# Decode attention over 65,536 keys on one core: from a tile framework with 2 MB tiles to hand-written engine programs with 8 MB tiles

## The chip, the core and the metric

The kernel runs on one core of a Trainium2 chip. The core has a matrix engine (TensorE, PE), a vector engine (VectorE, DVE), an activation engine (ScalarE, ACT), a general engine (GpSimd, POOL) and an engine that mostly issues transfers (SyncE, SP). Data comes from device memory (DRAM) into the on-chip buffer (SBUF, 128 partitions) through 16 DMA engines; matmul results land in PSUM, also on the chip. The metric is the device time of one execution in microseconds (us), the median of several runs.

## The reference

32 query heads in 8 groups of 4 share 8 key/value heads. Each head has one query of 128 numbers and looks at 65,536 keys.

```python
B, Hq, Hkv, Sq, Sk, D = 1, 32, 8, 1, 65536, 128      # all bfloat16
k = jnp.repeat(k, 4, axis=1)
v = jnp.repeat(v, 4, axis=1)
scores = jnp.einsum("bhqd,bhkd->bhqk", q, k) * D ** -0.5
p = _softmax(scores, axis=-1)
return jnp.einsum("bhqk,bhkd->bhqd", p, v)
```

Keys and values are 8 x 65536 x 128 x 2 bytes each, together 268.4 MB, and each byte is used once. The output is 8 KB.

## The kernel before

A tile framework orders the work: the program is written in sequence, and the framework puts in the waits between engines and recycles buffers out of pools.

**Tiles and loads.** The 65,536 rows of one group are 512 rows for each of 128 partitions. A tile is 64 rows for each partition, 16 KB a partition and 2 MB in all, so a group has KT = 8 key tiles and 8 value tiles. `k_load` (L117) and `v_load` (L209) issue them from SP into one pool of 8 buffers (`iopool`), keys and values in turn. In the key tensor a partition's rows lie 128 KB after those of the partition before; in the value tensor, which is cut in four parts first, 32 KB. The very last value tile is loaded in 4 pieces of 512 KB (`pieces=4`, L259).

**The order.** The outer loop runs over g = 0..8 (L251). In turn g it does, for s = 0..7, the key tile s of group g (`k_step`) and the value tile s of group g-1 (`v_step`), and then `softmax(g)`. So values run one group behind keys.

**k_step.** For each 16 rows of a key tile DVE transposes 32x32 blocks of 4-byte pairs into a new tile T (L128), and PE does four matmuls of 128x512 with a sparse query matrix `wq` as weights (L140), which add up in PSUM. After 32 matmuls ACT copies 128x512 scores from PSUM to `S_g` in SBUF (L148).

**softmax.** DVE takes the maximum (L153), PE and DVE bring it together and spread it (L157 to L171), ACT does exp with the sum (L175), PE transposes the weights in 16 pieces (L194) and ACT copies them into `ET` (L197).

**v_step.** PE multiplies 4 value rows at a time, 128x512, with 32 columns of `ET` as weights, in four column strips of PSUM in turn (L226). After the last tile of a group ACT copies the sums (L235), 4 matmuls, each run as two passes, pick the wanted parts (L238), DVE divides (L246), and ACT issues the store (L249).

`queries` fills `wq` for a group (L107), on POOL from group 1 on.

Of the kernel before, what the change touches and what calls it, by code (L numbers as in the profile page):

```python
# [8 lines left out]
ALU = mybir.AluOpType  # L9
# [3 lines left out]

NT = 64
NW = 16
# [3 lines left out]
def kernel(  # L19
# [11 lines left out]

    nc = tc.nc
    P = nc.NUM_PARTITIONS
    B, Hq, Sq, D = q.shape
    _, Hkv, Sk, _ = k.shape
    assert B == 1 and Sq == 1 and D == P  # L40
    HPG = Hq // Hkv
    assert HPG == 4 and HPG * Hkv == Hq
    R = Sk // P
    C = R // 4
    assert C == 8 * NW and R % NT == 0 and C % NT == 0
    NU = 4
    KT = R // NT
    WT = NT // NW
    SCALE = float(D) ** -0.5

    fp32 = mybir.dt.float32
    bf16 = mybir.dt.bfloat16

    const = ctx.enter_context(tc.tile_pool(name="const", bufs=1))
    iopool = ctx.enter_context(tc.tile_pool(name="iopool", bufs=8))
    tpool = ctx.enter_context(tc.tile_pool(name="tpool", bufs=4))
    spool = ctx.enter_context(tc.tile_pool(name="spool", bufs=2))
    epool = ctx.enter_context(tc.tile_pool(name="epool", bufs=2))
    opool = ctx.enter_context(tc.tile_pool(name="opool", bufs=2))
    stats = ctx.enter_context(tc.tile_pool(name="stats", bufs=2))  # L60
    psc = ctx.enter_context(tc.tile_pool(name="psc", bufs=3, space=bass.MemoryType.PSUM))
    pse = ctx.enter_context(tc.tile_pool(name="pse", bufs=2, space=bass.MemoryType.PSUM))
    psm = ctx.enter_context(tc.tile_pool(name="psm", bufs=1, space=bass.MemoryType.PSUM))
    pso = ctx.enter_context(tc.tile_pool(name="pso", bufs=2, space=bass.MemoryType.PSUM))


    qn = const.tile([P, D], bf16)
    for a in range(4):
        nc.scalar.dma_start(out=qn[32 * a:32 * a + 32, :], in_=q[0, :, 0, :])  # L69
    qx = const.tile([P, D], bf16)  # L70
    nc.vector.transpose(out=qx[:, :].bitcast(fp32), in_=qn[:, :].bitcast(fp32))

    qv = qx[:, :].rearrange("p (b h r) -> p b h r", b=2, r=2)

    ident = const.tile([P, P], fp32)
    make_identity(nc, ident[:, :])
    ident_bf = const.tile([P, P], bf16)
    nc.vector.tensor_copy(out=ident_bf[:, :], in_=ident[:, :])

    selx = const.tile([P, 32], fp32)  # L80
    nc.vector.tensor_reduce(
        out=selx[:, :], in_=ident[:, :].rearrange("p (j x) -> p x j", x=32), axis=AX.X, op=ALU.max
    )
    sel = const.tile([P, HPG], fp32)
    nc.vector.tensor_reduce(
        out=sel[:, :], in_=ident[:, :].rearrange("p (x h) -> p h x", h=HPG), axis=AX.X, op=ALU.max
    )
    one = const.tile([1, 1], fp32)
    nc.vector.memset(one[:, :], 1.0)

    Wq = []
    for x in range(2):
        wq = const.tile([P, 8 * 516], bf16, name=f"wq{x}")
        (nc.vector if x == 0 else nc.gpsimd).memset(wq[:, :], 0.0)
        Wq.append(wq)

    def queries(g):
        eng = nc.vector if g == 0 else nc.gpsimd  # L100
        wv = Wq[g % 2][:, :].rearrange("p (w x) -> p w x", x=516)
        for a in range(4):
            qd = slice(32 * a, 32 * a + 32)
            for b in range(2):
                for r in range(2):
                    at = 128 * (2 * b + r) + 32 * a
                    eng.tensor_copy(  # L107
                        out=wv[qd, :, at:at + HPG],
                        in_=qv[qd, b, g * HPG:(g + 1) * HPG, r].unsqueeze(1).broadcast_to([32, 8, HPG]),
                    )  # L110

    S_tiles, sc_tiles, ET_tiles, rl_tiles, o_tiles = {}, {}, {}, {}, {}

    def k_load(g, s):
        kn = iopool.tile([P, NT, D], bf16, name="kn", tag="io")
        src = k[0, g].rearrange("(p n) d -> p n d", p=P)
        nc.sync.dma_start(out=kn[:, :, :], in_=src[:, s * NT:(s + 1) * NT, :])  # L117
        return kn

    def k_step(g, s, kn):  # L120
        if s == 0:
            S_tiles[g] = spool.tile([P, NU, 4 * P], fp32, name="S_g")
        wq = Wq[g % 2]
        for x in range(WT):
            wg = s * WT + x
            nu, w = divmod(wg, 8)
            T = tpool.tile([P, NW * D], bf16, name="T")
            nc.vector.transpose(  # L128
                out=T[:, :].bitcast(fp32),
                in_=kn[:, x * NW:(x + 1) * NW, :].rearrange("p n d -> p (n d)").bitcast(fp32),  # L130
            )
            Tv = T[:, :].rearrange("p (n b i r) -> p n b i r", n=NW, b=2, r=2)
            if w == 0:
                sc_tiles[g] = psc.tile([P, 4 * P], fp32, name="sc")
            sc = sc_tiles[g]
            for b in range(2):
                for r in range(2):
                    bp = 2 * b + r
                    at = w * 512 + bp * 128
                    nc.tensor.matmul(  # L140
                        out=sc[:, :],
                        lhsT=wq[:, at:at + 128],
                        rhs=Tv[:, :, b, :, r],
                        start=(w == 0 and bp == 0),
                        stop=(w == 7 and bp == 3),
                    )
            if w == 7:
                nc.scalar.copy(out=S_tiles[g][:, nu, :], in_=sc[:, :])  # L148

    def softmax(g):  # L150
        S_g = S_tiles[g]
        mx = stats.tile([P, 1], fp32, name="mx")
        nc.vector.tensor_reduce(  # L153
            out=mx[:, :], in_=S_g[:, :, :].rearrange("p n c -> p (n c)"), axis=AX.X, op=ALU.max
        )
        psum_t = psm.tile([1, P], fp32, name="psum_t", tag="misc")
        nc.tensor.transpose(out=psum_t[:, :], in_=mx[:, :], identity=ident[:, :])  # L157
        m4 = stats.tile([1, HPG], fp32, name="m4")
        nc.vector.tensor_reduce(
            out=m4[:, :], in_=psum_t[:, :].rearrange("o (x h) -> o h x", h=HPG), axis=AX.X, op=ALU.max  # L160
        )
        mrow = stats.tile([1, P], fp32, name="mrow")
        nc.vector.tensor_scalar_mul(  # L163
            out=mrow[:, :].rearrange("o (x h) -> o x h", h=HPG),
            in0=m4[:, :].unsqueeze(1).broadcast_to([1, 32, HPG]),
            scalar1=-SCALE,
        )
        psum_b = psm.tile([P, 1], fp32, name="psum_b", tag="misc")
        nc.tensor.matmul(out=psum_b[:, :], lhsT=mrow[:, :], rhs=one[:, :], start=True, stop=True)  # L169
        nmb = stats.tile([P, 1], fp32, name="nmb")  # L170
        nc.vector.tensor_copy(out=nmb[:, :], in_=psum_b[:, :])  # L171

        E_g = epool.tile([P, NW, P], bf16, name="E_g")
        lsum = stats.tile([P, 1], fp32, name="lsum")
        nc.scalar.activation(  # L175
            out=E_g[:, :, :].rearrange("p c (i u) -> p u c i", u=NU),
            in_=S_g[:, :, :].rearrange("p u (c i) -> p u c i", c=NW),
            func=ACT.Exp,
            bias=nmb[:, 0:1],
            scale=SCALE,  # L180
            accum_out=lsum[:, 0:1],
        )
        psum_l = psm.tile([HPG, 1], fp32, name="psum_l", tag="misc")
        nc.tensor.matmul(out=psum_l[:, :], lhsT=sel[:, :], rhs=lsum[:, :], start=True, stop=True)  # L184
        rl = stats.tile([HPG, 1], fp32, name="rl")
        nc.vector.reciprocal(out=rl[:, :], in_=psum_l[:, :])  # L186
        rl_tiles[g] = rl

        ET = epool.tile([P, NW * P + 16], bf16, name="ET")
        nc.gpsimd.memset(ET[:, NW * P:], 0.0)  # L190
        for c4 in range(NW // 4):
            pe = pse.tile([P, 4, P], bf16, name="pe")
            for c in range(4):
                nc.tensor.transpose(  # L194
                    out=pe[:, c, :], in_=E_g[:, 4 * c4 + c, :], identity=ident_bf[:, :]
                )
            nc.scalar.copy(  # L197
                out=ET[:, :NW * P].rearrange("p (x c h) -> p c x h", c=NW, h=HPG)[:, 4 * c4:4 * c4 + 4],
                in_=pe[:, :, :].rearrange("p c (x h) -> p c x h", h=HPG),
            )  # L200
        ET_tiles[g] = ET

# [11 lines left out]
    def v_step(g, s, vb):  # L214
        if s == 0:
            o_tiles[g] = pso.tile([P, 4, D], fp32, name="psum_o")
# [34 lines left out]
    for g in range(Hkv + 1):  # L251
        if g < Hkv:
            queries(g)
# [38 lines left out]
```

## Time and profile before

| what | us |
|---|---|
| median of 3 runs (641.66 to 641.91) | 641.76 |
| span of the profiled execution, first to last instruction | 639.9 |
| PE busy / DVE busy / ACT busy in it | 409.9 / 326.1 / 81.2 |

The profile is one execution of its own; its span leaves out what lies before the first and after the last instruction. An engine's busy time is not by itself a reason for the time: what counts is what the last instruction waited for. The page cuts the span in 40 slices of 16 us; a digit is a share in tenths. The row PEclk gives the clock that was granted to PE, and GB/s what the 16 DMA engines moved. The chain of waits goes back from the last instruction to what released it, and so on to the start.

### The profile page before, as it was taken

How to read it: one execution, taken by the hardware profiler on the slowest of the kernel's cores; microseconds unless marked ns; L12 is line 12 of the kernel's file. 1: busy time of each engine (PE TensorE's matmuls, PEld its weight loads, DVE VectorE, ACT ScalarE, POOL GpSimd, SP SyncE). 2: the span in 40 equal slices, each digit the busy share in tenths (PEclk: the TensorE clock that was granted, in tenths of full speed). 3: DMA queues.
4: the chain of work that ended last, by engine and by line, in shares of the span. 5: the costliest groups of instructions: out<-in, count | busy, mean ns of one | idle time of the engine just before them, and what ended most of it. 6: DMA issues, size and time to landing. Idle time of an engine off the chain costs nothing.

```text
span 639.9 us, 5675 instructions
## 1 busy us (share of the span) xinstructions
PE 409.9 (64%) x2280; PEld 157.7 (25%) x2280; DVE 326.1 (51%) x326; ACT 81.2 (13%) x89; POOL 27.4 (4%) x127
## 2 busy tenths in 40 slices
PE   1996875666675765758657487564875558665554
PEld 0332321232222322223222132221322123221221
DVE  4996645455355553555534555435645356354300
ACT  0003100040000400013000220003100032000310
POOL 4002000200002000020000200002000000000000
PEclk9997878868878689887787877878878978879775
DMA  9999999999999999999999999999999999999994
GB/s 369 432 427 427 425 428 429 428 429 426 427 425 428 429 428 425 428 428 429 428 425 429 426 429 427 428 425 429 427 429 429 427 426 425 429 428 430 429 426 186
DMA packets 19146, 268.85 MB, mean 420 GB/s; under 512 B 2352, under 2 KB 2352, under 8 KB 2864
## 3 DMA queue, kind: packets, MB, share of 16 engines
q1 hardware_dynamic: 18864, 268.44, 98.8%
q8 instruction: 18, 0.29, 0.2%
q10 hardware_dynamic: 256, 0.04, 0.0%
q14 instruction: 8, 0.07, 0.0%
HBM read 268.47 MB, written 0.01 MB: 420 GB/s over the span
## 4 chain that ended last, share of the span: by engine, by line
DMA 82%; PE 9%; DVE 4%; issue 3%; ACT 1%; ACTq 0%; DVEq 0%; SPq 0%
DMA vb<-in_v_dram 43%; DMA kn<-in_k_dram 37%; PE sc L140 7%; DVE T L128 3%; DMA qn<-in_q_dram 1%; PE psum_o L226 1%; ACT E_g L175 1%; DVE mx L153 0%; PE psum_f L238 0%; DVE wq L107 0%; PE pe L194 0%; ACTq L69 0%; DVE o_out L246 0%; ACT o_sb L235 0%; ACT S_g L148 0%
## 5 line engine op out<-in xcount | busy, mean ns | idle before, releaser
L140 PE MATMUL sc<-T,wq 128*128 128x512 bf16 x1024 | 314.5, 457 | 159.9 <-DVE T L128 152.8
L128 DVE STREAM_TRANSPOSE T<-kn 128x1024 f32<-128x1024 f32 x256 | 296.3, 1211 | 211.8 <-DMA kn<-in_k_dram 209.3
L140 PEld LDWEIGHTS <-wq 128*128 128x128 bf16 x1024 | 112.5, 112 | 349.9 <-issue 244.7
L226 PE MATMUL psum_o<-vb,ET 128*32 128x512 bf16 x1024 | 73.3, 405 | 12.0 <-DMA vb<-in_v_dram 12.0
L148 ACT COPY S_g<-sc 128x512 f32<-128x512 f32 x32 | 18.7, 585 | 482.3 <-PE sc L140 482.3
L175 ACT ACTIVATE E_g<-S_g,nmb 128x2048 bf16<-128x2048 f32 x8 | 38.7, 4838 | 29.5 <-DVE nmb L171 29.5
L107 POOL COPY wq<-qx 32x32 bf16<-32x32 bf16 x112 | 22.4, 205 | 413.2 <-PE sc L140 402.7
L226 PEld LDWEIGHTS <-ET 128*32 128x32 bf16 x1024 | 23.7, 99 | 57.0 <-issue 43.2
L153 DVE TENSOR_REDUCE mx<-S_g 128x1 f32<-128x2048 f32 x8 | 18.3, 2286 | 20.5 <-ACT S_g L148 20.5
L184 PE MATMUL psum_l<-lsum,sel 128*4 128x1 f32 x16 | 1.5, 165 | 37.5 <-ACT E_g L175 37.5
L197 ACT COPY ET<-pe 128x512 bf16<-128x512 bf16 x32 | 17.8, 587 | 12.2 <-PE pe L194 12.2
L186 DVE RECIPROCAL rl<-psum_l 4x1 f32<-4x1 f32 x8 | 1.2, 155 | 33.7 <-PE psum_l L184 33.7
L194 PE MATMUL pe<-ident_bf,E_g 128*128 128x128 bf16 x128 | 17.5, 304 | 0.8 <-ACT ET L197 0.8
L246 DVE TENSOR_SCALAR o_out<-psum_f,rl 4x128 bf16<-4x128 f32 x8 | 2.6, 330 | 29.9 <-PE psum_f L238 29.9
L194 PEld LDWEIGHTS <-E_g 128*128 128x128 bf16 x128 | 13.6, 140 | 6.5 <-issue 6.1
L238 PE MATMUL psum_f<-o_sb,selx 128*4 128x128 f32 x64 | 9.1, 290 | 5.5 <-ACT o_sb L235 5.5
L184 PEld LDWEIGHTS psum_l<-lsum,sel 128*4 128x4 f32 x16 | 0.7, 84 | 38.6 <-ACT E_g L175 38.6
L235 ACT COPY o_sb<-psum_o 128x512 f32<-128x512 f32 x8 | 4.7, 585 | 27.4 <-PE psum_o L226 27.4
L238 PEld LDWEIGHTS psum_f<-o_sb,selx 128*4 128x4 f32 x64 | 5.1, 90 | 10.9 <-ACT o_sb L235 9.5
L157 PE MATMUL psum_t<-ident,mx 128*1 128x128 f32 x8 | 2.2, 270 | 6.8 <-DVE o_out L246 3.8
L169 PE MATMUL psum_b<-one,mrow 1*128 1x1 f32 x16 | 3.0, 256 | 5.0 <-DVE mrow L163 5.0
L190 POOL MEMSET ET<- 128x16 bf16 x8 | 0.9, 110 | 79.2 <-PE psum_o L226 78.8
(21 smaller groups left out, 20.9 us busy)
## 6 DMA issues: line engine op xcount, KB each, us to landing
kn<-in_k_dram SPq DMA_DIRECT2D x64, 2048.0 KB, 34.2
vb<-in_v_dram SPq DMA_DIRECT2D x63, 2048.0 KB, 34.2
vb<-in_v_dram SPq DMA_DIRECT2D x4, 512.0 KB, 27.0
out_dram<-o_out ACTq DMA_DIRECT2D x8, 1.0 KB
qn<-in_q_dram ACTq DMA_DIRECT2D x4, 8.0 KB, 8.4
```

What stands on the lines that cost most here:

```text
L107: eng.tensor_copy(out=wv[qd, :, at:at + HPG], in_=qv[qd, b, g * HPG:(g + 1) * HPG, r].unsqueeze(1).broadcast_to([32, 8, HPG]),)
L128: nc.vector.transpose(out=T[:, :].bitcast(fp32), in_=kn[:, x * NW:(x + 1) * NW, :].rearrange("p n d -> p (n d)").bitcast(fp32),)
L140: nc.tensor.matmul(out=sc[:, :], lhsT=wq[:, at:at + 128], rhs=Tv[:, :, b, :, r], start=(w == 0 and bp == 0), stop=(w == 7 and bp == 3),)
L148: nc.scalar.copy(out=S_tiles[g][:, nu, :], in_=sc[:, :])
L153: nc.vector.tensor_reduce(out=mx[:, :], in_=S_g[:, :, :].rearrange("p n c -> p (n c)"), axis=AX.X, op=ALU.max)
L169: nc.tensor.matmul(out=psum_b[:, :], lhsT=mrow[:, :], rhs=one[:, :], start=True, stop=True)
L175: nc.scalar.activation(out=E_g[:, :, :].rearrange("p c (i u) -> p u c i", u=NU), in_=S_g[:, :, :].rearrange("p u (c i) -> p u c i", c=NW), ...
L194: nc.tensor.transpose(out=pe[:, c, :], in_=E_g[:, 4 * c4 + c, :], identity=ident_bf[:, :])
L197: nc.scalar.copy(out=ET[:, :NW * P].rearrange("p (x c h) -> p c x h", c=NW, h=HPG)[:, 4 * c4:4 * c4 + 4], in_=pe[:, :, :].rearrange("p c ( ...
L226: nc.tensor.matmul(out=psum_o[qd, :, :], lhsT=ET[:, col:col + 32], rhs=vb[:, x:x + 4, :], start=(j < 4), stop=(j >= R // 4 - 4),)
L235: nc.scalar.copy(out=o_sb[:, :, :], in_=psum_o[:, :, :])
L238: nc.tensor.matmul(out=psum_f[:, :], lhsT=selx[:, HPG * c:HPG * c + HPG], rhs=o_sb[:, c, :], start=(c == 0), stop=(c == 3),)
```

## The change

The framework's order is replaced by five programs, one for each engine, written out with semaphores inside one critical section.

- Loads are 8 MB: NT = 256 rows, 64 KB a partition, two tiles of keys and two of values a group. There are three buffers. `bufA` takes the first half of a group's keys, `bufB` the second, `bufC` both halves of the values of the group before; at the end A and B take the last group's values. SP issues each load behind a wait for the work that frees its buffer (`kdone`, `vdone`). Keys and values both have partitions 128 KB apart.
- The last value tile comes in 7 pieces of 128, 64, 32, 16, 8, 4 and 4 rows, each with a semaphore. The first two are used as before, four rows at a time; the next three one row at a time in four column strips (`quads`); the last two one row at a time straight into the result (`singles`).
- Keys are transposed in place, half a tile (128x8192 pairs) in one instruction (`turn`).
- The four blocks of 128x512 scores stay in four PSUM banks; one exp reads them all. The weights are turned by one DVE transpose in place of 16 PE transposes and 4 ACT copies.
- `wq` is one copy of shifted windows in place of two large ones, filled by 4 POOL copies a group.
- PE's instructions for groups 1 to 7 stand in a loop of 7 turns that counts semaphores down (`take`).

```diff
-NT = 64
-NW = 16
+G = 8
+H = 4
+P = 128
+D = 128
+NT = 256
+W = 8
+C = 16
+SLIDE = P + 4 * (W - 1)
+PIECES = (128, 64, 32, 16, 8, 4, 4)
...
+    bufA, bufB, bufC = (sbuf(n, (P, NT * D), bf16) for n in ("bufA", "bufB", "bufC"))
+    wq = sbuf("wq", (P, 4 * SLIDE), bf16)
+    E = sbuf("E", (P, 4 * 512 + 32), bf16)
...
+    sc = psum("sc", (P, 4 * 512))
+    psum_o = psum("psum_o", (P, 512))
+    psum_s = psum("psum_s", (P, 512))
+    psum_f = psum("psum_f", (P, 512))
+    misc = psum("misc", (P, 512))
...
+        def load(buf, src, s, semaphore, lo=0, n=NT):
+            sp.dma_start(
+                out=buf[:, lo * D:(lo + n) * D],
+                in_=src[:, s * half + lo * D:s * half + (lo + n) * D],
+            ).then_inc(semaphore, 16)
+        load(bufA, kr[0], 0, sA)
+        load(bufB, kr[0], 1, sB)
+        load(bufC, vr[0], 0, sC)
+        for g in range(1, G):
+            sp.wait_ge(kdone, 2 * g - 1)
+            load(bufA, kr[g], 0, sA)
+            if g == 1:
+                sp.wait_ge(kdone, 2)
+                load(bufB, kr[1], 1, sB)
+                sp.wait_ge(vdone, 1)
+                load(bufC, vr[0], 1, sC)
+                continue
+            sp.wait_ge(vdone, 2 * (g - 1))
+            load(bufC, vr[g - 1], 0, sC)
+            sp.wait_ge(kdone, 2 * g)
+            load(bufB, kr[g], 1, sB)
+            sp.wait_ge(vdone, 2 * (g - 1) + 1)
+            load(bufC, vr[g - 1], 1, sC)
+        sp.wait_ge(kdone, 2 * G - 1)
+        load(bufA, vr[G - 1], 0, sA)
+        sp.wait_ge(kdone, 2 * G)
+        at = 0
+        for x, n in enumerate(PIECES):
+            load(bufB, vr[G - 1], 1, sP[x], at, n)
+            at += n
...
+        def turn(buf, x):
+            kv = buf[:, x * half // 2:(x + 1) * half // 2].bitcast(fp32)
+            dve.transpose(out=kv, in_=kv).then_inc(kt, 1)
...
+        n_pes = 0
+        for g in range(G):
+            dve.wait_ge(sA, 16 * (g + 1))
+            turn(bufA, 0)
+            turn(bufA, 1)
+            dve.wait_ge(sB, 16 * (g + 1))
+            turn(bufB, 0)
+            turn(bufB, 1)
+            dve.wait_ge(kdone, 2 * (g + 1))
+            dve.tensor_reduce(out=mx[:, :], in_=sc[:, :], axis=AX.X, op=ALU.max).then_inc(mxs, 1)
+            if g > 0:
+                n_pes += 1
+                dve.wait_ge(pes, n_pes)
+                dve.tensor_scalar_mul(
+                    out=o_out[:, (g - 1) * D:g * D], in0=psum_f[0:H, 0:D], scalar1=rl[:, 0:1]
+                ).then_inc(outs, 1)
+            n_pes += 1
+            dve.wait_ge(pes, n_pes)
+            after(dve.tensor_reduce(
+                out=m4[:, :], in_=misc[0:1, 0:P].rearrange("o (x h) -> o h x", h=H), axis=AX.X, op=ALU.max
+            ))
+            dve.tensor_scalar_mul(
+                out=mrow[:, :].rearrange("o (x h) -> o x h", h=H),
+                in0=m4[:, :].unsqueeze(1).broadcast_to([1, 32, H]),
+                scalar1=-SCALE,
+            ).then_inc(mxs, 1)
+            n_pes += 1
+            dve.wait_ge(pes, n_pes)
+            dve.tensor_copy(out=nmb[:, :], in_=misc[:, P:P + 1]).then_inc(nms, 1)
+            dve.wait_ge(exd, g + 2)
+            dve.transpose(out=E[:, 0:2048], in_=E[:, 0:2048]).then_inc(ets, 1)
+            n_pes += 1
+            dve.wait_ge(pes, n_pes)
+            dve.reciprocal(out=rl[:, :], in_=misc[0:H, P + 4:P + 5]).then_inc(dl, 1)
...
+        for g in range(G):
+            if g > 0:
+                act.wait_ge(vdone, 2 * g)
+                act.copy(out=o_sb[:, :], in_=psum_o[:, :]).then_inc(ocp, 1)
+            act.wait_ge(nms, g + 1)
+            act.activation(
+                out=E[:, 0:2048], in_=sc[:, :], func=ACT.Exp, bias=nmb[:, 0:1], scale=SCALE,
+                accum_out=lsum[:, 0:1],
+            ).then_inc(exd, 1)
+            if g > 0:
+                store(g - 1)
...
+        def take(semaphore, n=1):
+            pe.wait_ge(semaphore, n).then_inc(semaphore, -n)
+        def scores(buf, x, s):
+            take(kt)
+            bank = sc[:, (2 * s + x) * 512:(2 * s + x + 1) * 512]
+            T = buf[:, x * half // 2:(x + 1) * half // 2].rearrange(
+                "p (c w b i r) -> p w b r c i", c=C, w=W, b=2, r=2
             )
...
+            for w in range(W):
+                for b in range(2):
+                    for r in range(2):
+                        at = (2 * b + r) * SLIDE + 4 * (W - 1 - w)
+                        last = pe.matmul(
+                            out=bank, lhsT=wq[:, at:at + P], rhs=T[:, w, b, r],
+                            start=(w + b + r == 0), stop=(w == W - 1 and b + r == 2),
+                        )
+            return last
...
+        def stream(buf, s, lo, n, end):
+            for row in range(lo, lo + n, 4):
+                j = row // 4
+                qd = slice(32 * (j % 4), 32 * (j % 4) + 32)
+                at = column(s, row) // 32 * 32
+                last = pe.matmul(
+                    out=psum_o[qd, :], lhsT=E[:, at:at + 32], rhs=buf[:, row * D:(row + 4) * D],
+                    start=(s == 0 and j < 4), stop=(s == 1 and row >= end - 16),
                 )
...
+            return last
...
+        def pick(start, stop):
+            for x in range(4):
+                last = pe.matmul(
+                    out=psum_f[0:H, 0:D], lhsT=selx[:, H * x:H * x + H], rhs=o_sb[:, x * D:(x + 1) * D],
+                    start=(start and x == 0), stop=(stop and x == 3),
                 )
...
+            return last
+        def maxima():
+            take(mxs)
+            pe.transpose(out=misc[0:1, 0:P], in_=mx[:, :], identity=ident[:, :]).then_inc(pes, 1)
+            take(mxs)
+            pe.matmul(
+                out=misc[:, P:P + 1], lhsT=mrow[:, :], rhs=one[:, :], start=True, stop=True
+            ).then_inc(pes, 1)
+        def sums():
+            take(ets)
+            pe.matmul(
+                out=misc[0:H, P + 4:P + 5], lhsT=sel[:, :], rhs=lsum[:, :], start=True, stop=True
+            ).then_inc(pes, 1)
...
+        take(wqs, 4)
+        scores(bufA, 0, 0)
+        scores(bufA, 1, 0).then_inc(kdone, 1)
+        scores(bufB, 0, 1)
+        scores(bufB, 1, 1).then_inc(kdone, 1)
+        maxima()
+        with pe.Fori(1, G):
+            sums()
+            take(sC, 16)
+            stream(bufC, 0, 0, NT, NT).then_inc(vdone, 1)
+            take(wqs, 4)
+            scores(bufA, 0, 0)
+            scores(bufA, 1, 0).then_inc(kdone, 1)
+            scores(bufB, 0, 1)
+            take(sC, 16)
+            stream(bufC, 1, 0, NT, NT).then_inc(vdone, 1)
+            scores(bufB, 1, 1).then_inc(kdone, 1)
+            take(ocp)
+            pick(True, True).then_inc(pes, 1)
+            maxima()
+        sums()
+        pe.wait_ge(sA, 16 * (G + 1))
+        stream(bufA, 0, 0, NT, NT).then_inc(vdone, 1)
+        at = 0
+        for x in range(2):
+            pe.wait_ge(sP[x], 16)
+            last = stream(bufB, 1, at, PIECES[x], PIECES[0] + PIECES[1])
+            at += PIECES[x]
+        last.then_inc(vdone, 1)
+        def quads(lo, n, start, stop):
+            for row in range(lo, lo + n):
+                qd = slice(32 * (row % 4), 32 * (row % 4) + 32)
+                col = column(1, row)
+                last = pe.matmul(
+                    out=psum_s[qd, 0:D], lhsT=E[:, col:col + 32], rhs=bufB[:, row * D:(row + 1) * D],
+                    start=(start and row < lo + 4), stop=(stop and row >= lo + n - 4),
+                )
+            return last
+        def singles(lo, n, stop):
+            for row in range(lo, lo + n):
+                col = column(1, row)
+                last = pe.matmul(
+                    out=psum_f[0:H, 0:D], lhsT=E[:, col:col + H], rhs=bufB[:, row * D:(row + 1) * D],
+                    start=False, stop=(stop and row == lo + n - 1),
+                )
+            return last
+        pe.wait_ge(sP[2], 16)
+        quads(at, PIECES[2], True, False)
+        at += PIECES[2]
+        pe.wait_ge(ocp, 1)
+        pick(True, False)
+        pe.wait_ge(sP[3], 16)
+        quads(at, PIECES[3], False, False)
+        at += PIECES[3]
+        pe.wait_ge(sP[4], 16)
+        quads(at, PIECES[4], False, True).then_inc(vdone, 1)
+        at += PIECES[4]
+        pe.wait_ge(sP[5], 16)
+        singles(at, PIECES[5], False)
+        at += PIECES[5]
+        pe.wait_ge(ocp, 2)
+        pe.matmul(out=psum_f[0:H, 0:D], lhsT=selq[:, 0:H], rhs=s_sb[:, :], start=False, stop=False)
+        pe.wait_ge(sP[6], 16)
+        singles(at, PIECES[6], True).then_inc(pes, 1)
```

More of the change, by code (lines that the diff above doesn't have):

```diff
@@ L5 @@
 from concourse import mybir
-from concourse.masks import make_identity
 from concourse._compat import with_exitstack
@@ L52 @@
     bf16 = mybir.dt.bfloat16
[L54 to L130, printed above, removed]
-            )
[L132 to L195, printed above, removed]
-                )
[L197 to L201, printed above, removed]
@@ L251, with sbuf @@
-    for g in range(Hkv + 1):
-        if g < Hkv:
-            queries(g)
-        for s in range(KT):
-            if g < Hkv:
-                k_step(g, s, k_load(g, s))
-            if g > 0:
-                last = g == Hkv and s == KT - 1
-                v_step(g - 1, s, v_load(g - 1, s, pieces=4 if last else 1))
-        if g < Hkv:
-            softmax(g)
+    pe, dve, act, pool, sp = nc.tensor, nc.vector, nc.scalar, nc.gpsimd, nc.sync
+    def sbuf(name, shape, dtype=fp32):
+        return nc.alloc_sbuf_tensor(name, list(shape), dtype)
@@ new lines @@
+    ident = sbuf("ident", (P, P))
+    s64 = sbuf("s64", (P, 64))
+    selx = sbuf("selx", (P, 4 * H))
+    selq = sbuf("selq", (P, 32))
+    sel = sbuf("sel", (P, H))
+    one = sbuf("one", (1, 1))
+    mx = sbuf("mx", (P, 1))
+    m4 = sbuf("m4", (1, H))
+    mrow = sbuf("mrow", (1, P))
+    nmb = sbuf("nmb", (P, 1))
+    lsum = sbuf("lsum", (P, 1))
+    rl = sbuf("rl", (H, 1))
+    sc = psum("sc", (P, 4 * 512))
+    psum_o = psum("psum_o", (P, 512))
+    psum_s = psum("psum_s", (P, 512))
+    psum_f = psum("psum_f", (P, 512))
@@ new lines, with sem @@
+    misc = psum("misc", (P, 512))
+    def sem(name):
+        return tc.alloc_semaphore(name)
+    sA, sB, sC = sem("sA"), sem("sB"), sem("sC")
+    sP = [sem(f"sP{x}") for x in range(len(PIECES))]
+    sQ = sem("sQ")
+    sS = sem("sS")
+    kt = sem("kt")
+    kdone = sem("kdone")
+    vdone = sem("vdone")
+    wqs = sem("wqs")
+    cst = sem("cst")
+    mxs = sem("mxs")
+    pes = sem("pes")
+    nms = sem("nms")
+    qps = sem("qps")
+    exd = sem("exd")
+    ets = sem("ets")
+    ocp = sem("ocp")
```

151 lines of the change are left out of this document (96 added, 55 removed).

## The prediction

> **What bounds the kernel now.** I read the page's slices first, then its chain of waits, then windows over chosen stretches.
>
> ```profile
> span 639.9 us, 5675 instructions
> PEclk9997878868878689887787877878878978879775
> GB/s 369 432 427 427 425 428 429 428 429 426 427 425 428 429 428 425 428 428 429 428 425 429 426 429 427 428 425 429 427 429 429 427 426 425 429 428 430 429 426 186
> q1 hardware_dynamic: 18864, 268.44, 98.8%
> q8 instruction: 18, 0.29, 0.2%
> DMA 82%; PE 9%; DVE 4%; issue 3%; ACT 1%; ACTq 0%; DVEq 0%; SPq 0%
> ```
>
> From the second slice to the last but one, transfers never let up. 268.44 MB at 427 GB/s are 628.7 us of the 639.9. The chain agrees: 82% of it is DMA. No compute engine matters until the last slice, so an edit to PE, DVE or ACT alone is worth nothing; only four things can move the time: the start, the rate, a gap between loads, and the tail. The rate in windows (columns: us of the window, busy us of each engine with its number of instructions, clock, DMA share, GB/s):
>
> ```profile
> core 0: us, PE busy (x) PEld busy (x) DVE busy (x) ACT busy (x) POOL busy (x), PEclk, DMA share, GB/s
> 20.00:40.00 20.00, 18.77 (x77) 7.25 (x76) 20.00 (x19) 1.17 (x2) 0.00 (x0) 1.00 1.01 431
> 300.00:500.00 200.00, 131.71 (x727) 49.70 (x725) 99.23 (x92) 21.77 (x25) 6.71 (x34) 0.83 1.01 428
> 624.00:630.00 6.00, 2.64 (x24) 0.96 (x27) 0.00 (x0) 0.00 (x0) 0.00 (x0) 0.50 0.96 391
> 630.00:634.30 4.30, 2.86 (x28) 0.78 (x20) 0.00 (x0) 0.00 (x0) 0.00 (x0) 0.50 0.37 148
> ```
>
> At the end the 16 DMA engines do not finish together. At 428 GB/s the last two windows would carry 4408 KB; they carry 391 x 6 + 148 x 4.3 = 2982 KB. The missing 1426 KB are 3.3 us of full rate. The tail, from the timeline (start, duration, engine, line):
>
> ```profile
> 624.32 1.90 PE L226 MATMUL psum_o<-vb,ET 128*32 128x512 bf16 x16 [3.85 <-DMA vb<-in_v_dram]
> ...
> 631.74 0.62 PE L226 MATMUL psum_o<-vb,ET 128*32 128x512 bf16 x4 [0.15 <-DMA vb<-in_v_dram]
> ...
> 633.00 0.62 PE L226 MATMUL psum_o<-vb,ET 128*32 128x512 bf16 x4 [0.65 <-DMA vb<-in_v_dram]
> ...
> 634.25 0.62 PE L226 MATMUL psum_o<-vb,ET 128*32 128x512 bf16 x4 [0.64 <-DMA vb<-in_v_dram]
> ...
> 634.91 0.59 ACT L235 COPY o_sb<-psum_o 128x512 f32<-128x512 f32 x1 [24.54 <-PE psum_o L226]
> ...
> 635.55 1.87 PE L238 MATMUL psum_f<-o_sb,selx 128*4 128x128 f32 x8 [0.69 <-ACT o_sb L235]
> 637.46 0.34 DVE L246 TENSOR_SCALAR o_out<-psum_f,rl 4x128 bf16<-4x128 f32 x1 [29.86 <-PE psum_f L238]
> 637.83 0.26 ACTq L249 DMA_DIRECT2D out_dram<-o_out  x1
> ```
>
> The last quarter tile releases PE at 634.25. From there to the end of the span are 5.65 us: matmuls, copy, pick, divide, and 2.07 from the store's issue to the end. So the profiled time is 634.25 + 5.65, and the median of the runs, 641.76, is 1.86 above this span; I carry that 1.86 over.
>
> **Part 1: fewer, larger loads.** Before, 64 + 63 whole tiles and 4 quarters are 131 loads; after, 31 whole tiles and 7 pieces are 38. What does one load cost beyond its bytes? Two sizes are in the trace. A 2.097 MB tile at 431 GB/s takes 4.866 us. The 0.524 MB quarters released PE at 631.74, 633.00 and 634.25, so 1.255 us each. The 1.573 MB between the two sizes take 3.611 us, which is 435.6 GB/s; 0.524 MB at that rate are 1.204 us; 0.051 us are left for the load itself, its 128 rows and its completion. With 428 GB/s for the tile the same steps give 0.040. I take 0.051, since in 20 to 40 us the DMA engines still ran evenly, as the quarters' spacing does. 93 loads fewer: -4.7 us. This supposes that a 64 KB row costs no more beside its bytes than a 16 KB row. If the row is cut into 16 KB pieces on its way, most of it is gone and the term is 0; as the other end I take -6, for a price that is a quarter above the row's.
>
> The page "SBUF — State Buffer" of the Trainium skill (section "The DMA setup-cost knee") gives every transfer a fixed cost of about 2 us, which is mostly completion. By that rule 93 fewer loads would save some 186 us as an estimate. The trace disagrees for a full queue: the rows above leave 0.05 us, because the next load's data move while one completes.
>
> **Part 2: three buffers in place of eight.** The queue holds fewer loads; a gap opens if a buffer is not free when the load before it ends. What the waits in the new SP program depend on:
>
> ```profile
> L128 DVE STREAM_TRANSPOSE T<-kn 128x1024 f32<-128x1024 f32 x256 | 296.3, 1211 | 211.8 <-DMA kn<-in_k_dram 209.3
> L71 DVE STREAM_TRANSPOSE qx<-qn 128x64 f32<-128x64 f32 x1 | 0.2, 245 | 7.6 <-DMA qn<-in_q_dram 7.6
> L153 DVE TENSOR_REDUCE mx<-S_g 128x1 f32<-128x2048 f32 x8 | 18.3, 2286 | 20.5 <-ACT S_g L148 20.5
> L175 ACT ACTIVATE E_g<-S_g,nmb 128x2048 bf16<-128x2048 f32 x8 | 38.7, 4838 | 29.5 <-DVE nmb L171 29.5
> L107 POOL COPY wq<-qx 32x32 bf16<-32x32 bf16 x112 | 22.4, 205 | 413.2 <-PE sc L140 402.7
> ```
>
> ```profile
> 15.39 0.14 PEld L140 LDWEIGHTS <-wq 128*128 128x128 bf16 x1 [0.28 <-issue]
> 15.82 0.14 PEld L140 LDWEIGHTS <-wq 128*128 128x128 bf16 x1 [0.28 <-issue]
> ...
> 519.70 2.29 DVE L153 TENSOR_REDUCE mx<-S_g 128x1 f32<-128x2048 f32 x1 [3.67 <-ACT S_g L148]
> ...
> 529.04 0.15 DVE L186 RECIPROCAL rl<-psum_l 4x1 f32<-4x1 f32 x1 [4.07 <-PE psum_l L184]
> ...
> 535.79 3.64 PE L140 MATMUL sc<-T,wq 128*128 128x512 bf16 x16
> 539.36 1.05 PE L226 MATMUL psum_o<-vb,ET 128*32 128x512 bf16 x16
> ```
>
> A transpose of 8192 pairs: from 64 pairs in 0.245 us to 1024 in 1.211 a pair adds 1.006 ns, so 0.245 + 8128 x 1.006 ns = 8.4 us; the other end is eight short ones, 9.7. I take 9. A score matmul takes 3.64 / 16 = 0.23 us at the better clock, 0.43 at the spacing of the early weight loads; half a tile (32) is 7.3 or 13.8. A value tile (64) is 4.2 (from 1.05 / 16), or 7.6 (from 1.90 / 16). From the maximum to the reciprocal, softmax took 529.19 - 519.70 = 9.5 us; its DVE transpose of the weights has no row, and I bound it by 1.2 (as many bytes as a 1024-pair one) and 2.3 (as many elements as the maximum): 12 in all.
>
> An 8.389 MB load takes 19.4. Count from the landing of A(g), and let each engine work in program order. DVE turns A by 9 and 18. The first value half lands at 19.4 and PE has it by 23.6; scores of A end at 38.2, and A is needed again at 58.2. B lands at 38.8, is turned by 48 and 57; its first half is scored by 55. The second value half lands at 58.2 and is used by 62.4; C is needed again at 77.6. B's second half is scored by 70; B is needed at 97. Softmax ends by 82, the next value half lands at 97. So each buffer is free 15 to 27 us early, and the queue does not run dry: 0. DVE's wait for the scores (`kdone`) holds back the next group's transposes, which wait for data until 77.6 anyway; SP's waits hold only loads that no one needs sooner; POOL's `wq` copies (4 x 0.2) lie under the value half. One place is tighter: the last pieces wait for B, free at 70 or, at half clock, at 66 + 13.8 = 80; they should start at 77.6. That is 0, at most +2.4.
>
> At the start A needs 19.4 us to land before any work, and B and C are already queued; A must be free at 58.2 after its start and, by the same durations at half clock, is so at 19.4 + 18 + 13.8 = 51. The longer wait of the first work is covered by the queue; if it were not, each us late would be a us lost. POOL's constants and the query load lie under it as well.
>
> **Part 3: the work that leaves.** The 32 score copies, the 16 weight transposes and 4 copies a group, `S_g` and the pool bookkeeping go: 0, since DMA covers them all. The loop adds branches and may load PE's instructions anew at each turn. The q8 row has 18 such transfers of 0.29 MB in all, and they share the DMA engines with the data. Bounds: the unevenness of 3.3 us vanishes or doubles. I take 0.
>
> **Part 4: the tail.** PE's program after the 64-row piece is short matmuls. The clock is 0.50 in the last windows. For a `quads` matmul (32 weight columns, 128 columns moved) the nearest row is 1.90 / 16 = 0.119 us for four times the columns; a quarter of that is 0.03. I take 0.06, as the weight load doesn't shrink with the columns. After the 32-row piece 1.05 MB are still to come, 2.4 us and four loads, so it lands 2.6 before the last one. Then 32 x 0.06 end at -0.7; `pick` (1.87) at +1.2; 24 more quads at +2.6; the copy of 128 columns, between nothing and the 0.59 for 512, 0.3, at +2.9; the `selq` matmul, two passes of 1.87 / 8, at +3.4; four `singles` at 0.06 at +3.6; divide 0.34 and store 2.07, with hops: +6.2. Against 5.65 that is +0.5. Ends: 2.9 if only the last four matmuls, the divide and the store remain; with 0.119 for 64 matmuls, 10: -2.8 to +4.3.
>
> **Sum.** 639.9 - 4.7 + 0 + 0 + 0.5 = 635.7 us of span, and 637.6 us of time. The start is taken as unchanged: SP issues its first load first, as before.
>
> **The rivals.**
>
> (a) *The row is cut on its way, or the rate doesn't rise.* The 16 KB rows of before say nothing of 64 KB ones. Then 641.8 + 0.5 = 642.3 us, no measurable difference.
>
> (b) *PE becomes the bound, at half clock.* In the new loop PE's work is a chain: values, A, B, values, B, softmax. For it speaks that the PEclk row hardly reaches 9 after the start and that in the new order PE idles for 10 us at a time. At 0.43 us a period is 128 x 0.43 + 128 x 0.119 + 12 for softmax + 1.9 for `pick` + 0.8 = 85 us, against 77.6 for its four loads: 7 turns x 7.4 = 52, so 690 us. It decides from about 0.39 us a matmul on. Against it: bursts of 32 to 64 matmuls, and 0.23 in the burst at 535.79; then the period is 53 us. The Trainium skill's "TensorE: Matmul & The Clock Gate" (Part 1) says that the clock halves after about 3.4 us of idling and comes back after 3.4 us of work. The 0.83 in the window 300 to 500 agrees with clocks in between; by that rule only the start of each burst is slow.
>
> (c) *The queue runs dry at each hand-over*, if the wait before a load passes only after the load ahead has landed. The first slice carries 369 GB/s for 427, so it loses 16 x 58 / 427 = 2.2 us, of which some 1.4 are left after the first issue at 0.73 (the row below). 31 of these are 43 us: 638 + 43 = 681 us. The walk above speaks against it, by 15 us and more at each buffer.
>
> ```profile
> 0.73 17.79 SPq L117 DMA_DIRECT2D kn<-in_k_dram  x9
> ```
>
> **How the numbers follow.** Forecast 0.73, (a) 0.13, (b) 0.05, (c) 0.05, and 0.04 for a slower end or start that I don't see. The forecast's own terms reach from 639.9 - 6 - 3.3 - 2.8 to 639.9 + 2.4 + 3.3 + 4.3 in span if all fell together, which they hardly will; half of that around 637.6 is 631.5 to 642, and (a) lies at 642.3: the range is 631.5 to 643. A measurement of this kernel tells about 0.2% from no change, 640.5 to 643.0. Of the forecast 0.05 lies there, and of (a) 0.10: faster 0.68, same 0.15, slower 0.17 from (b), (c), the rest of (a) and what I don't see.
>
> **What would show it.** Right: middle slices at 430 GB/s or more, as high as the 431 here, with no dip at the loads' ends; kdone's last scores of a tile over 10 us ahead of the next landing in the same buffer; last landing near 629.5; about 6 us from it to the end. Wrong: slices still at 427 (rival a); PE busy without pause and dips in the GB/s row (b); a dip every 19 us (c); a tail of 8 us or more, with `quads` still running after the last landing.

## The result, and the profile after

The changed kernel takes 631.34 us, the median of 4 runs (630.22 to 631.47), beside 641.74 for the kernel before: a ratio of 0.9834, with a 95% interval of 0.982 to 0.9848. So it is 10.4 us faster, where 4.2 were forecast, and lies 0.2 us below the forecast range. In two later comparisons its median was 630.02 and 630.03. The kernel before lay between 641.74 and 641.90 each time, so times of different comparisons can be set side by side to about 1.3 us, which is how far the changed kernel's own medians lie apart.

The page of the changed kernel:

```profile
span 629.7 us, 4775 instructions
PEclk9999769885788758787587975869659696597976
GB/s 400 400 466 401 462 404 459 408 455 412 454 412 454 412 454 412 454 412 450 416 450 416 450 416 450 416 450 416 450 416 450 416 454 416 450 425 441 433 407 239
q1 hardware_dynamic: 5472, 268.44, 98.8%
q8 instruction: 4, 0.07, 0.0%
```

The q1 row had 18864 packets. 131 loads of 128 rows, with one small packet for each of 16 DMA engines at the end of each load, make 131 x 144 = 18864; 38 x 144 are 5472. So a 64 KB row travels as one packet and is not cut; the trace lists 3968 packets of 65,536 bytes, which are 31 loads of 128 rows. The q8 row fell from 18 to 4: the loop's instructions are not transferred anew in each turn. Do not read the GB/s row slice by slice here: 450 and 416 in turn come from counting. A packet is counted whole in the slice in which it starts, and a slice of 16 us holds 6 or 7 starts of these large packets on each engine. Long windows show the rate (us of the window, busy us by engine, clock, DMA share, GB/s):

```profile
100.00:300.00 200.00, 111.95 (x711) 48.08 (x709) 107.24 (x32) 7.93 (x9) 2.28 (x12) 0.78 1.00 433
300.00:500.00 200.00, 104.13 (x671) 44.62 (x672) 104.44 (x26) 5.29 (x6) 1.52 (x8) 0.76 1.00 434
618.00:622.00 4.00, 1.90 (x16) 0.46 (x16) 0.00 (x0) 0.17 (x1) 0.00 (x0) 0.50 0.98 399
622.00:624.90 2.90, 2.53 (x49) 1.90 (x50) 0.00 (x0) 0.42 (x1) 0.00 (x0) 0.50 0.43 153
```

The rate is 433 to 434 in place of 427 to 428. The start is as before: the first data packet starts at 1.9 us, at 1.7 before. At the end the missing bytes, against 434, are 35 x 4 + 281 x 2.9 = 955 KB or 2.2 us, where they were 3.3; part of that is now the seven small pieces. Some 0.5 us of each of the two lie between the end of the last packet (624.43 here, 633.78 before) and the end of the window. The end of the timeline (start, duration, engine, line):

```profile
622.37 1.04 PE L377 MATMUL psum_s<-bufB,E 128*32 128x128 bf16 x32 [0.58 <-DMA bufB<-in_v_dram]
623.20 1.49 PE L322 MATMUL psum_f<-o_sb,selx 128*4 128x128 f32 x6
...
624.70 1.05 PE L377 MATMUL psum_s<-bufB,E 128*32 128x128 bf16 x18
625.54 0.63 PE L386 MATMUL psum_f<-bufB,E 128*4 128x128 bf16 x4
625.81 0.27 ACT L274 COPY s_sb<-psum_s 128x128 f32<-128x128 f32 x1 [3.39 <-PE psum_s L377]
626.13 0.54 PE L407 MATMUL psum_f<-s_sb,selq 128*4 128x128 f32 x2
626.51 0.39 PE L386 MATMUL psum_f<-bufB,E 128*4 128x128 bf16 x4
626.93 0.34 DVE L245 TENSOR_SCALAR o_out<-psum_f,rl 4x128 bf16<-4x128 f32 x1 [21.28 <-PE psum_f L386]
627.30 0.26 ACTq L256 DMA_DIRECT2D out_dram<-o_out  x1
```

From 622.37 on PE never waits for data: only the first row has idle time before it. The last piece lands at 624.9; the span ends at 629.7, 4.8 us later.

### The profile page after: what moved, and what is told of

Read it like the earlier page. It is cut to its first block, busy times and chain, and to the rows that moved or that the text cites. A ratio compares the mean times of both kernels' runs of the same rounds, so it can differ in the third digit from the quotient of the medians.

```text
span 629.7 us, 4775 instructions
## 1 busy us (share of the span) xinstructions
PE 337.6 (54%) x2203; PEld 145.1 (23%) x2203; DVE 322.8 (51%) x93; ACT 23.0 (4%) x27; POOL 7.9 (1%) x43
## 5 line engine op out<-in xcount | busy, mean ns | idle before, releaser
L203 DVE STREAM_TRANSPOSE bufB<-bufB 128x8192 f32<-128x8192 f32 x16 | 138.4, 8690 | 130.9 <-DMA bufB<-in_k_dram 130.9
L297 PE MATMUL sc<-bufB,wq 128*128 128x512 bf16 x512 | 128.9, 413 | 59.1 <-PEq L284 59.1
L203 DVE STREAM_TRANSPOSE bufA<-bufA 128x8192 f32<-128x8192 f32 x16 | 138.2, 8673 | 18.3 <-DMA bufA<-in_k_dram 18.3
L314 PE MATMUL psum_o<-bufC,E 128*32 128x512 bf16 x896 | 65.5, 457 | 124.9 <-PEq L284 124.9
L297 PE MATMUL sc<-bufA,wq 128*128 128x512 bf16 x512 | 116.2, 385 | 30.2 <-PEq L284 30.2
L297 PEld LDWEIGHTS sc<-bufB,wq 128*128 128x128 bf16 x512 | 51.4, 103 | 136.1 <-issue 86.6
L297 PEld LDWEIGHTS sc<-bufA,wq 128*128 128x128 bf16 x512 | 49.0, 97 | 96.6 <-issue 38.5
L214 DVE TENSOR_REDUCE mx<-sc 128x1 f32<-128x2048 f32 x8 | 18.3, 2292 | 97.5 <-PE sc L297 97.5
L314 PEld LDWEIGHTS psum_o<-bufC,E 128*32 128x32 bf16 x896 | 29.5, 112 | 158.1 <-issue 145.9
L236 DVE STREAM_TRANSPOSE E<-E 128x2048 bf16<-128x2048 bf16 x8 | 18.5, 2311 | 17.0 <-ACT E L265 17.0
## 6 DMA issues: line engine op xcount, KB each, us to landing
bufB<-in_v_dram SPq DMA_DIRECT2D x1, 4096.0 KB, 18.2
bufC<-in_v_dram SPq DMA_DIRECT2D x14, 34.9
bufA<-in_k_dram SPq DMA_DIRECT2D x8, 37.6
```

The lines of the kernel that those rows point to most:

```text
L203: dve.transpose(out=kv, in_=kv).then_inc(kt, 1)
L214: dve.tensor_reduce(out=mx[:, :], in_=sc[:, :], axis=AX.X, op=ALU.max).then_inc(mxs, 1)
L236: dve.transpose(out=E[:, 0:2048], in_=E[:, 0:2048]).then_inc(ets, 1)
L297: last = pe.matmul(out=bank, lhsT=wq[:, at:at + P], rhs=T[:, w, b, r], start=(w + b + r == 0), stop=(w == W - 1 and b + r == 2),)
L314: last = pe.matmul(out=psum_o[qd, :], lhsT=E[:, at:at + 32], rhs=buf[:, row * D:(row + 4) * D], start=(s == 0 and j < 4), stop=(s == 1 and ...
```

## The experiments

All but one start from the changed kernel. Times are medians; q8 is the number of instruction transfers on the page.

| kernel | us | loads | rows (1000) | q8 |
|---|---|---|---|---|
| before | 641.8 | 131 | 16.8 | 18 |
| changed | 631.34, 630.02, 630.03 | 38 | 4.9 | 4 |
| unrolled | 633.65 | 38 | 4.9 | 17 |
| loads_2mb | 637.73 | 131 | 16.8 | 4 |
| loads_4mb | 633.26 | 69 | 8.8 | 4 |
| loads_4mb_16kb_rows | 638.32 | 69 | 16.8 | 4 |
| loads_2mb_unrolled | 640.54 | 131 | 16.8 | 17 |
| before_4mb | 637.45 | 71 | 9.1 | 18 |
| tail_quarters | 633.56 | 35 | 4.5 | 4 |
| tail_sixteens | 632.08 | 38 | 4.9 | 4 |
| tail_early_pick | 629.76, 630.17 | 38 | 4.9 | 5 |

### Is it the loads, or their rows?

Each 8 MB load is issued as several, into the same place:

```diff
-            sp.dma_start(
-                out=buf[:, lo * D:(lo + n) * D],
...
+            step = NT // 4 if n == NT else n
+            for x in range(lo, lo + n, step):
+                sp.dma_start(
+                    out=buf[:, x * D:(x + step) * D],
...
-            dve.wait_ge(sA, 16 * (g + 1))
+            dve.wait_ge(sA, 64 * (g + 1))
...
```

> Each 8 MB load is issued as four loads of 2 MB with 16 KB rows into the same buffer, back to back; the loop and the tail stay. 93 loads more. Theory (price per load as the prediction sized it, 0.051 us): +4.7, 636.1. If it was sized too low and the whole gain in rate is this price (0.065 to 0.07): +6.0 to +6.5, 637.3 to 637.8. Rival (the rate rose because ACT, POOL and the pool bookkeeping are gone, not because of the loads): 631.3, slices at 433 GB/s as in the changed kernel.

With 2 in place of 4:

> Each 8 MB load as two loads of 4 MB with 32 KB rows. 31 loads and as many rows again more. By either price, per load or per row, a third of what four loads of 2 MB cost: +1.6 at 0.051, +2.1 at 0.068, so 632.9 to 633.4. If rows over some length bring nothing more: 631.3.

And two loads again, each of which takes every second 16 KB of a row:

```diff
...
+            to = buf[:, :].rearrange("p (a b x) -> p a b x", a=2, b=2)
+            frm = src[:, s * half:(s + 1) * half].rearrange("p (a b x) -> p a b x", a=2, b=2)
+            for x in range(2):
+                sp.dma_start(out=to[:, :, x, :], in_=frm[:, :, x, :]).then_inc(semaphore, 16)
...
```

> Each 8 MB load as two loads of 4 MB, each of which takes every second 16 KB of a partition's 64 KB: rows as short as with 2 MB loads, loads as few as with 4 MB ones. Theory A (each row costs): the time of the kernel with four 2 MB loads, +4.7 to +6.5. Theory B (each load's completion costs): the time of the kernel with two 4 MB loads, +1.6 to +2.1.

637.73 (ratio to before 0.9934, 0.9918 to 0.9951), 633.26 (0.9874, 0.9857 to 0.989) and 638.32 (0.9946, 0.9929 to 0.9963). The third kernel decides: with as few loads as the second it takes the time of the first, whose rows it shares (0.6 us more). So the price is for the row, not for the load, and completions cost nothing that shows. The windows say the same; first the kernel with 2 MB loads, then the one with 4 MB loads of 16 KB rows:

```profile
300.00:500.00 200.00, 102.52 (x666) 43.95 (x666) 101.89 (x25) 5.29 (x6) 1.52 (x8) 0.76 1.01 428
```

```profile
300.00:500.00 200.00, 102.94 (x666) 44.01 (x666) 101.97 (x25) 5.29 (x6) 1.52 (x8) 0.76 1.01 428
```

428 GB/s, as before the change, with the new work on all other engines: the rate has nothing to do with what ACT, POOL or the pools no longer do. The price: (637.73 - 633.26) / 62 = 0.072 us for 128 rows, which are 8 on each of 16 DMA engines, 9 ns a row. For 93 loads that is 6.7 us.

That last step takes the price between 16 and 32 KB as good up to 64 KB, and the packets in the traces bear it out. With the bytes of each packet spread over its duration, the stretch from 100 to 600 us has 428.3, 431.6 and 433.4 GB/s with rows of 16, 32 and 64 KB. That is 612.1, 1214.7 and 2419.3 ns for a row on one of 16 engines, so two rows take 9.6 and 10.1 ns longer than one of twice their length.

The Trainium skill, "DMA: Bandwidth & Descriptors" (section "Why small descriptors are slow (HBM only)"), has a fixed cost of about 3 cycles a packet and treats it as a matter of 256 bytes. That there is a fixed cost fits these runs; the size and the range do not. At that section's 32 bytes a cycle, 3 cycles are 0.6% of a 16 KB row, as an estimate; measured are about 9 ns, 1.5% of it. The 2 us of the page of the Trainium skill that the prediction quotes do not show at all once the queue holds a next load.

The same part alone, in the kernel before: larger tiles in fewer buffers.

```diff
-NT = 64
+NT = 128
...
-    iopool = ctx.enter_context(tc.tile_pool(name="iopool", bufs=8))
+    iopool = ctx.enter_context(tc.tile_pool(name="iopool", bufs=4))
...
-                v_step(g - 1, s, v_load(g - 1, s, pieces=4 if last else 1))
+                v_step(g - 1, s, v_load(g - 1, s, pieces=8 if last else 1))
```

> One part of the change alone, in the kernel before: tiles of 128 rows (4 MB, 32 KB a partition) in four buffers in place of 64 rows in eight; the last tile in eight pieces of 512 KB, so that the end is as it was. 71 loads in place of 131, at half the number of long rows. Theory (each row costs some 8 ns on its DMA engine, as between four 2 MB loads and two 4 MB loads in the changed kernel, 4.5 us): 641.8 - 4.4 = 637.4, q8 still about 18 and the uneven finish as before. Rival 1 (the framework's own waits or PE's work set the time there): 641.8. Rival 2 (four large buffers run dry where eight small ones did not): above 642, with dips in the GB/s row.

637.45 (0.9933, 0.9916 to 0.995), as expected. Three constants give that kernel 4.4 of the 10.4 us.

### The loop

```diff
-        with pe.Fori(1, G):
+        for _ in range(1, G):
```

> PE's loop of 7 turns is written out; everything else is the changed kernel. Theory: the instruction transfers (q8: 18 before, 4 after) run on the data's DMA engines and each puts one engine behind, so they made the uneven finish of before. Then q8 is back at 15 to 20, the last DMA engines finish late again (the last 4 us before the last landing well under 400 GB/s) and the time is 632.8 to 634.5, 1.5 to 3 us above the changed kernel's 631.34. Rival: the uneven finish came from the eight buffers or the two spacings of rows; then the time stays within 0.7 us of 631.34 whatever q8 shows.

633.65 (0.9871, 0.9855 to 0.9888): 2.3 us above the changed kernel's 631.34, 3.6 above 630.03. Its page and the windows before its last landing:

```profile
q8 instruction: 17, 0.28, 0.2%
```

```profile
620.00:624.00 4.00, 1.45 (x16) 0.47 (x16) 0.00 (x0) 0.00 (x0) 0.00 (x0) 0.50 0.87 343
624.00:627.70 3.70, 3.29 (x61) 1.94 (x54) 0.00 (x0) 0.58 (x1) 0.00 (x0) 0.50 0.29 112
```

Against 434 GB/s they lack 91 x 4 + 322 x 3.7 = 1555 KB, 3.6 us; the changed kernel lacked 2.2. In windows of 200 us in the middle both show 434, which is too coarse for what the transfers do. The list of DMA packets in the traces shows it. An instruction transfer is one packet of 16 KB, 0.9 to 1.1 us long, on one DMA engine, and each engine ends its part of a load with a small packet of its own. For the load that ends at about 605 us these small packets start within 1.8 us in the changed kernel, 12 of the 16 within 0.3 us. In the unrolled kernel they start within 3.4 us, and 9 engines are 1.3 to 3.4 us behind the first, whose packet starts at 603 us in both. So the transfers put the engines that carry them behind, and a load is complete only with the engine that is furthest behind.

> Both at once: four loads of 2 MB with 16 KB rows in place of each 8 MB load, and PE's loop written out. This gives back the row length and the instruction transfers of the kernel before and keeps the new tail, the three buffers and the new work of the engines. Theory (the whole gain is rows, instruction transfers and a tail shorter by 0.8 us): 641.8 - 0.8 = 641, or the changed kernel + 6.4 + 2.3 = 640. Rival (something else, such as ACT's or POOL's missing work, brought part of it): below 638.5.

640.54 (0.9982, 0.9973 to 0.9991), 2.8 above the kernel with 2 MB loads and the loop. With the old rows and the old instruction transfers, 1.3 of the 641.82 us measured beside it are left to the tail and all else.

The last landings in the profiles, one of each kernel, separate the data's part from the tail's. The last piece lands at 634.2 us in the kernel before and at 634.3 in this one, at 631.5 with the old rows and the loop, at 627.7 with the new rows and no loop, and at 624.9 and 624.4 in the changed kernel. So longer rows bring the landing forward by 6.7 to 7.1 us and the loop by 2.8 to 3.2, and the buffers, the spacing of the rows and the other engines' work by nothing that shows.

### The tail

```diff
-PIECES = (128, 64, 32, 16, 8, 4, 4)
+PIECES = (64, 64, 64, 64)
-        for x in range(2):
+        for x in range(4):
             pe.wait_ge(sP[x], 16)
-            last = stream(bufB, 1, at, PIECES[x], PIECES[0] + PIECES[1])
+            last = stream(bufB, 1, at, PIECES[x], NT)
...
         pe.wait_ge(ocp, 1)
-        pick(True, False)
...
+        pick(True, True).then_inc(pes, 1)
```

> The last value tile in four pieces of 64 rows, all used four rows at a time as before, with one copy of the sums and one pick after them; no quads, no singles. The prediction's working (seven pieces make the tail 0.5 us longer and three more loads cost 0.2): 0.7 us below the changed kernel. The other theory (the short pieces take work off the end): after the last landing remain 16 matmuls in 1.9 us at half clock, 0.6 copy, 1.9 pick, 0.3 divide, 2.4 store, 7.1 with the hops, in place of 4.85; so 2 us above the changed kernel.

633.56 (0.9871, 0.9856 to 0.9886), 3.5 above the changed kernel beside it. The prediction's figure does not apply to it, though, against what I expected: its last piece has 64 rows, and that of the kernel before had 16. So the old tail again, with PIECES = (64, 64, 64, 16, 16, 16, 16):

> The tail of the kernel before in the changed kernel: the last value tile in 7 pieces of 64, 64, 64 and four times 16 rows, all used four rows at a time, then one copy and one pick. As many pieces as in the changed kernel, and a last piece of 16 rows as in the kernel before (the kernel with four pieces of 64 rows had four times that). The prediction put the new tail 0.5 us above the old one, so 0.5 us below the changed kernel. From the traces of after: 4 matmuls 0.6, copy 0.6, pick 1.9, divide 0.3, store 2.4 are 5.9 with the hops, against 4.85 in the profile of after and 3.8 in its second one: 1 to 2 us above the changed kernel.

632.08 (0.9851, 0.9836 to 0.9866), 2.05 above the 630.03 beside it. The end of its timeline:

```profile
624.34 0.62 PE L312 MATMUL psum_o<-bufB,E 128*32 128x512 bf16 x4 [0.62 <-DMA bufB<-in_v_dram]
625.00 0.59 ACT L272 COPY o_sb<-psum_o 128x512 f32<-128x512 f32 x1 [22.77 <-PE psum_o L312]
625.64 1.87 PE L320 MATMUL psum_f<-o_sb,selx 128*4 128x128 f32 x8 [0.69 <-ACT o_sb L272]
627.55 0.34 DVE L245 TENSOR_SCALAR o_out<-psum_f,rl 4x128 bf16<-4x128 f32 x1 [22.45 <-PE psum_f L320]
```

and, of the changed kernel's third profile, the span, the window from 622 us to its last landing, and the timeline:

```profile
span 627.9 us, 4775 instructions
```

```profile
622.00:624.40 2.40, 2.40 (x68) 2.04 (x68) 0.00 (x0) 0.15 (x1) 0.00 (x0) 0.81 0.33 116
```

```profile
621.91 1.04 PE L377 MATMUL psum_s<-bufB,E 128*32 128x128 bf16 x32 [0.60 <-DMA bufB<-in_v_dram]
...
623.59 0.60 PE L377 MATMUL psum_s<-bufB,E 128*32 128x128 bf16 x18
624.19 0.38 PE L386 MATMUL psum_f<-bufB,E 128*4 128x128 bf16 x4
...
624.79 0.39 PE L386 MATMUL psum_f<-bufB,E 128*4 128x128 bf16 x4
```

The old tail runs 6.0 us from the landing at 624.34 to its span's end at 630.3, and in it the copy and the pick come after the last data. In the new one they overlap the last pieces. From the last landing to the end the changed kernel takes 4.8 us in its first profile and 3.5 in this one. The same 18 quads take 0.60 here and 1.05 in the first profile: the clock was 0.50 in the first profile's window, and 0.81 in this one's. So its end seems to depend on whether PE's clock comes back in time. That is argued from these profiles and not tried by itself; together with the last landing, 0.4 us later in the first profile, it fits the 1.3 us between its medians.

A last idea moves `pick` ahead of the quads, where PE idled:

```diff
-PIECES = (128, 64, 32, 16, 8, 4, 4)
+PIECES = (128, 32, 48, 32, 8, 4, 4)
...
+        pe.wait_ge(ocp, 1)
+        pick(True, False)
         pe.wait_ge(sP[2], 16)
         quads(at, PIECES[2], True, False)
         at += PIECES[2]
-        pe.wait_ge(ocp, 1)
-        pick(True, False)
```

> Pieces of 128, 32, 48, 32, 8, 4 and 4 rows, and pick stands ahead of the first quads, in time in which PE idled. In the changed kernel PE works without a pause from 622.4 to 626.9 while the last piece lands at 624.85; with pick's 1.5 to 1.9 us out of that stretch and 24 more quads in it (0.8 us) the end comes 0.5 to 1 us earlier: 0.1% below the changed kernel, at the edge of what can be told. Rival (the last landing sets the end, not PE): no change.

> The early pick once more, beside the changed kernel on one chip, to tell the two apart: 0.3 us below it in the first call. What is asked is whether the runs lie closer together (629.5 to 629.8 against 629.5 to 631.0), as they should if PE's clock at the end no longer matters because PE is not late.

> The changed kernel itself, for comparing the other kernels of this call on one chip: 631.3.

> The changed kernel beside these two: 630.0 to 631.4, by the clock that PE has in the last 5 us.

629.76 beside 630.02 (ratios to before 0.9813, 0.9799 to 0.9826, and 0.9822, 0.9809 to 0.9836), then 630.17 beside 630.03 (0.9817, 0.9804 to 0.983, and 0.9823, 0.9809 to 0.9836). No difference that can be told. The second time its runs reached from 629.62 to 630.45, so the closer runs of the first time did not come back. A miss: taking this work out of the last stretch changed nothing that can be told, which is what the rival forecast. The rival's reason, that the last landing sets the end, is not shown by it: in this kernel's first profile PE's last four matmuls start at 624.67, behind the copy of the quads' sums and the matmul on it, and the last piece had landed at 624.4.

## Why the prediction was off

The sum was -4.7 + 0 + 0 + 0.5, so -4.2. Three of its four terms were off, all in the same direction: the price of the loads, the instruction transfers, which were put at nothing, and the tail.

**What bounds the kernel** was right: transfers without a pause before and after, and only rate, unevenness and tail moved the time.

**Part 1, fewer and larger loads**, had the right kind of cost and too small a size, and it left open whether the load, its rows or its completion has the price: -4.7 forecast, -6.7 by the price of 0.072 us (6.4 to 7.7 by the kernel with 2 MB loads against the changed one's three medians). The 0.051 was a small difference of two large numbers. A quarter tile was put at 1.255 us from the spacing of the last landings, with a window beside it that showed 148 GB/s, so part of the DMA engines had already finished; and 431 GB/s came from a window of 20 us, where 428 holds over 200. Both are too coarse for a difference of 0.05. Rows, not loads, are the unit, as the supposition there had it. That the spacing of the last landings was unfit is argued from the window; that the price is 0.072 is shown.

**Part 2, three buffers**, was right. The longest waits are SP's own, and they cost nothing (the first two lines are SP's waits: us in all, times, the longest; the next two the us from issue to landing):

```profile
SPq L112 <- PE psum_o L314: 344.0, 13, 34.0
SPq L112 <- PE sc L297: 240.8, 16, 45.6
...
bufC<-in_v_dram SPq DMA_DIRECT2D x14, 34.9
bufA<-in_k_dram SPq DMA_DIRECT2D x8, 37.6
L203 DVE STREAM_TRANSPOSE bufB<-bufB 128x8192 f32<-128x8192 f32 x16 | 138.4, 8690 | 130.9 <-DMA bufB<-in_k_dram 130.9
L236 DVE STREAM_TRANSPOSE E<-E 128x2048 bf16<-128x2048 bf16 x8 | 18.5, 2311 | 17.0 <-ACT E L265 17.0
```

A load of 19.4 us lands 34.9 or 37.6 after its issue in the median, so it waited 15.5 to 18.2 in the queue; the shortest wait of an 8 MB load after the first was 12.8. The walk had buffers free 15 to 27 us early. The half-tile transpose takes 8.7 (8.4 worked out, 9 taken), and that of the weights 2.3, its upper bound.

**Part 3, the work that leaves**, is the step that failed. The row with 18 instruction transfers and the 3.3 us of uneven finish were both in view, the loop was named as something that may bring more of them, and the term was still set to 0, between bounds of 3.3 either way. The loop keeps its instructions: -2.3 to -3.6 by the unrolled kernel, -2.8 with 2 MB loads.

**Part 4, the tail**, had the wrong sign: +0.5 forecast, -2.05 by the old tail put into the changed kernel. 32 quads at half clock took 1.04 us in all, 0.033 each and so the bound from a quarter of the columns, not the 0.06 taken; and in the third profile the clock came back during the burst. From the last landing to the end are 4.8 us in the first profile, and 3.5 in the third, where the working had 6.2. `pick` overlaps the pieces that are still landing, as the working had it.

The three, -6.7, -2.8 and -2.05, make 11.6. The store takes back 0.3 of it: 2.4 us from its issue at 627.30 to the end, against 2.07 before; why, no run shows. That leaves 11.3, against 10.4 to 11.9 measured.

**The range** reaches too low by its own working. It takes half of 6 + 3.3 + 2.8 off 637.6, though 637.6 already holds 4.7 of the 6 and the 0.5 of the tail; counted from the forecast, half of the reach ends at 633.6. So the measured time lies further from what the prediction allowed for than the 0.2 us below 631.5 let it seem.

**The rivals.** (a) falls with the packets of the q1 row and 433 GB/s. (b) falls too: the clock was 0.76 to 0.78 in the middle, yet PE was busy in only 112 and 104 of 200 us. By its own sum it decides from 0.37 us a matmul on, not 0.39. (c) falls with the 12.8 us and more in the queue.

## What to carry to other kernels

Where transfers bound a kernel, count the rows on the busiest DMA engine and give each its price, 9 ns here: 16 KB rows still paid 1.5% for it, and fewer loads alone bring nothing when a next one is queued. Then look at what else rides on the same DMA engines: a program that fits in a loop leaves them to the data. At the end let copies and sums run while the last small pieces land, and get the price of a short instruction from a burst of short ones.

## What was not expected

Thirteen instruction transfers of 16 KB, 0.08% of the bytes, cost 2.3 to 3.6 us, since a load is complete only when the slowest of 16 DMA engines is. And the rate with 64 KB rows, 434 GB/s over 200 us, comes close to the ceiling of 435 that "DMA: Bandwidth & Descriptors" of the Trainium skill works out (section "Where 436 GB/s comes from").
